# One GpSimd transfer for u, loads ahead of the ramp, and a new order of steps in a fused RWKV and MLP kernel

## The chip, the cores and the metric

The kernel runs on one core of a Trainium2 chip. Its time is device microseconds from the start to the end of one execution. The core has five engines that run side by side, each with its own in-order queue: PE (TensorE, matmuls; its weight loads are listed as PEld), DVE (VectorE), ACT (ScalarE), POOL (GpSimd) and SP (SyncE, which here only issues DMAs). They meet through semaphores.

## What is computed

For 4 batches, 8 heads, 768 time steps and a head size of 48, a linear attention with decay runs through time; its output, 3072 rows of 384, goes through two matrices with a leaky ReLU between them:

```python
for t in range(S):
    cur = np.einsum('bhd,bhe->bhde', u[None] * kt, vt)
    y[:, :, t] = np.einsum('bhd,bhde->bhe', rt, state + cur)
    state = w[None, :, :, None] * state + np.einsum('bhd,bhe->bhde', kt, vt)
x = y.transpose(0, 2, 1, 3).reshape(B * S, H * D)
h = x @ w_in                        # 384 -> 2048
out = np.maximum(0.01 * h, h) @ w_out   # 2048 -> 384
```

## The kernel before

Time is cut into 24 stages of 128 steps (six per batch). Within a stage the recurrence is written as matrix products: the keys and queries are scaled by powers of w, their products (128x128 per head) are masked, and the state is carried from stage to stage. Two stages make a pair (0 to 11), which is 256 rows of x for the two big products.

The program is written out as a list, `ORDER`, of some 880 short step names. A step adds one or a few instructions to the queue of its engine; the list is read once from left to right, so each engine executes its own steps in the order of the list, and every dependence becomes a semaphore wait. The figure behind an `@` names the PSUM bank (of eight) that a PE step writes; a step that takes over a bank waits for the last reader of the step that had it. `RINGS` holds the numbers of buffers: the second is the number of buffers of the transposed keys and queries, `tp`.

The steps by letter, n being a stage and m a pair:

| step | engine | line | what |
|---|---|---|---|
| p0 ... p32 | all | 336 | entries of the list `first`: setting up |
| q | DVE | 373 | zeroes the padding of a qk buffer |
| F | PE | 376 | one product of ones, written to a bank and read by nobody |
| r, k, v | POOL | 267 | load of a stage (cast to bf16 on the way), one DMA each |
| i, w | POOL | 281, 285 | quarter of w_in, of w_out |
| P | DVE | 388 | scales queries and keys by the tables qtab and ktab; for stage 0 in two halves, P0.1 the keys, P0.0 the queries |
| T, C | PE, ACT | 408, 422 | transposes half of it on PE, copies it out of PSUM (stages 0 to 7) |
| X | SP | 402 | transposes by DMA (stages 8 to 23) |
| D, V | DVE | 428, 551 | the part with u for stages 0 to 5: product of keys and queries, and v scaled by its sums |
| E, f, R, L | DVE, POOL | 433 to 459 | the same part for stages 6 to 23: products with u_tab and r, their sums, and a diagonal tile by an affine select on POOL |
| A, M, m, N | PE, DVE, ACT | 467 to 509 | scores, masked (DVE, or ACT copy and DVE mask; from stage 6 a predicated copy over L's tile) |
| K, B, W | PE, DVE | 521 to 570 | keys times values, next state |
| Y, O | PE, ACT | 575, 618 | outputs of the stage, copied as x, transposed |
| J, j | PE, ACT | 650, 664 | 256 columns of h for a pair: six matmuls with 256 moving columns, eviction with the leaky ReLU; eight per pair |
| G, g | PE, ACT | 627, 642 | 512 columns of h for one stage alone: twelve matmuls with 128 moving columns, eviction of the same size; not in the list before |
| t, b, Z, z | DVE, PE | 701 to 766 | the product with w_out in seven half-size products per pair (sums of blocks on DVE, products, combination on ACT and DVE) |
| o | SP, ACT | 690 | stores 128 rows |

The steps of `first` that matter here: p0 loads w as a row, p1 loads u as a row (ACT's queue), p2 and p3 load r and k of stage 0 in fp32 on SP's and ACT's queues (into r0_f and k0_f), p4 to p7 load w and u as columns; p9 is the ramp (an iota on POOL), from which DVE makes kexp (p13), qexp (p14), ident (p15) and mask (p17); p10 sets the ones. p21 spreads w over 128 partitions by a product with a column of ones, p22 takes its logarithm, p24 and p23 make ktab and qtab from it with kexp and qexp. For u, p20 casts the row to bf16, p25 spreads it by a product and p26 copies it to u_tab, which E reads.

PE executes, in the list before, p21, p25, eleven F, T0.1, T0.0, three F, A0, and then stages 1 to 3 with further F between; the first J follows after Y1. POOL executes p9, r3, k3, k1, r1, k2, r2, i1, v0, k5, r5, and so on; L7 stands behind 25 stage loads.

Of the kernel before, what the change touches and what calls it, by code (L numbers as in the profile page):

```python
# [16 lines left out]
HD = H * D  # L17
# [6 lines left out]
RINGS = (6, 7, 6, 6, 6, 3, 3, 8, 14, 14)  # L24
# [8 lines left out]
F1.128.5@4 F1.512.8@2 p24 F1.256.12@0 k2 F1.512.15@7 P0.1 F1.256.4@0 F1.512.16@2 p17 r2 p27 p15 p23 p19 q5  # L33
F1.512.4@0 q4 q3 F1.512.6@7 P0.0 i1 p28 F1.256.9@0 p16 T0.1@2 v0 T0.0@0 F1.512.12@3 C0.1 p32 p31 F1.512.7@4 q1
F1.512.0@3 k5 C0.0 P1 p29 A0@23 D0 p30 r5 F1.512.5@0 q2 M0.0 F1.256.16@7 F1.512.19@6 T1.0@0 v1 P2 F1.128.2@4
F1.256.18@5 F1.512.9@2 C1.0 F1.256.6@7 P3 F1.512.13@6 T1.1@2 v2 M0.1 F1.256.14@0 T3.0@4 C1.1 T2.1@0 T3.1@5 C3.0
v3 D1 A1@23 C2.1 M1.0 i0 C3.1 K0@4 F1.256.3@0 T2.0@2 r4 V0 F1.256.2@0 C2.0 B0 Y0@0 m1.1 k6 P5 F1.256.8@2 A3@45
p26 D2 F1.128.3@7 F1.256.11@6 k4 K1@2 N1.1 D3 T5.1@3 V1 A2@67 r6 C5.1 T5.0@1 M3.1 O0 Y1@3 r7 C5.0 B1 K3@0 M2 O1
K2@5 k7 J0.3@1 v4 V2 A5@23 j0.3 B2 J0.1@6 i3 m5.1 M3.0 J0.0@7 V3 i2 D5 Y2@1 k8 E6 N5.1 Y3@5 O2 P4 v5 j0.1 B3
J0.2@1 O3 P6 v6 T4.1@6 j0.2 J1.3@0 j0.0 w3 T4.0@1 J1.0@3 C4.1 w2 P7 C4.0 J1.1@7 M5.0 w0 A4@45 D4 j1.1 T6.0@6 v7  # L40
f6 T6.1@1 j1.3 M4 T7.0@2 J1.2@7 j1.0 w1 C6.1 K4@0 J1.7@3 r13 C6.0 V4 J0.7@1 E7 j1.7 k9 W3 f7 T7.1@4 B4 j0.7
J1.6@3 R7 C7.0 J0.5@5 R6 j1.6 L7 b0.2 Y4@6 C7.1 j0.5 L6 A7@01 A6@23 O4 W4 K5@4 J0.4@5 V5 M7 J0.6@6 j0.4 r10 Y5@4
j0.6 r8 J1.5@5 b0.0 O5 r11 J1.4@6 b0.1 J2.2@4 M6 r9 j1.4 J2.5@0 j1.2 v8 j2.2 b0.3 J2.7@1 j1.5 k11 K6@6 J2.3@7
b1.0 k10 J2.4@2 B6 b1.1 J2.1@3 v9 b1.2 Y7@4 v11 Y6@5 E8 t0 J2.6@6 O6 k13 O7 Z0.0@5 t2 j2.5 k12 Z1.0@4 j2.7 t1
j2.3 J3.2@0 k14 z0.0 E9 j2.1 K7@1 Z0.1@7 t3 v13 j2.6 J3.1@3 j2.4 f8 r12 b1.3 Z1.1@6 j3.1 P8 v12 Z0.2 P9 Z0.3@2
P11 X9 z0.2 j3.2 f9 Z0.4 B7 z1.1 z1.0 E11 J3.3@3 z0.1 X8 W7 R9 K8@0 Z1.2 j3.3 f11 L9 Z1.3@1 z1.2 Z1.4 P13 Z0.5
R8 X13 z1.4 J3.5@3 L8 B8 z0.4 Z1.5 X11 z1.3 r19 R11 Z0.6 W8 r22 P10 A9@01 j3.5 z1.5 Z1.6 X10 M9 z0.6 L11 A8@56
J2.0@3 r15 M8 J3.6@0 j2.0 v16 J3.4@1 E12 f12 v10 Y9@3 E10 P12 Y8@5 O9 r18 b2.0 X12 J3.0@6 j3.4 E13 O8 Z2.0@3 k17
z0.3 j3.6 f10 f13 J4.7@5 o2 z1.6 R10 k16 j3.0 J4.1@4 z0.5 R13 L10 J3.7@2 j4.1 K12@1 k15 J4.4@0 j3.7 B12 z2.0
J4.0@4 b3.0 j4.7 k19 b2.1 A10@12 j4.0 A11@56 r14 Z2.1@7 j4.4 M11 L13 Z2.2 M10 J4.6@4 k21 J4.2@0 j4.6 b2.3 k23  # L50
J4.5@5 z2.1 j4.2 b2.2 J4.3@6 j4.5 K9@4 z2.2 Z2.3@2 j4.3 B9 R12 A13@01 A12@45 M13 L12 Z3.0@6 Z2.4 z3.0 r21 W9 M12
Z2.5 v20 K10@0 Z3.1@1 B10 v18 z2.5 Y12@4 z3.1 Y10@5 W10 O12 b3.1 Y13@0 v14 Y11@7 P15 O13 K13@4 k18 O10 b4.0 Z3.2
O11 z2.3 J6.0@0 v21 E15 z3.2 z2.4 J6.6@5 f15 v17 b4.1 Z3.3@7 B13 r17 J5.1@2 b3.2 Z2.6 r16 P14 j6.0 b3.3 j5.1
J5.3@4 b4.2 Z3.4 j5.3 P18 J6.2@0 E17 E14 J5.0@2 b4.3 j6.2 J5.5@4 R15 z2.6 o5 f14 Z3.5 L15 X14 j5.5 R14 J6.3@0
j5.0 z3.4 E19 v15 P16 J6.1@3 X15 f19 L14 Z4.0@4 j6.1 Z3.6 o1 W13 X16 J6.4@2 P17 z3.6 j6.6 P19 J5.7@3 j6.4 E18 o7
K14@6 f18 Z4.1@5 j5.7 X18 z3.5 B14 j6.3 J5.4@2 z3.3 z4.0 E16 z4.1 J5.6@3 o4 W14 o0 Z4.2 j5.6 X19 A14@01 z4.2
# [107 lines left out]
def bass_rwkv5_eagle__then__act_leaky_relu_kernel(  # L164
# [13 lines left out]
    def SB(name, shape, dt=BF16):  # L178
        return ctx.enter_context(nc.sbuf_tensor(name, shape, dt))
# [9 lines left out]
    u_row = SB("u_row", [1, HD], FP32)  # L189
# [5 lines left out]
    k0_f = SB("k0_f", [128, HD], FP32)  # L195
    r0_f = SB("r0_f", [128, HD], FP32)
# [7 lines left out]
    u_row16 = SB("u_row16", [1, HD])  # L204
    one_row16 = SB("one_row16", [1, 128])
# [37 lines left out]

    def k_of(n):
        return k_sb[:, n % NRK, :] if n else k0_f[:, :]

    def r_of(n):
        return r_sb[:, n % NRK, :] if n else r0_f[:, :]
# [10 lines left out]
    def load_first(which):  # L259
        src = {"k": k, "r": r}[which][0].rearrange("h t d -> t h d")[0:L, :, :]  # L260
        dst = {"k": k0_f, "r": r0_f}[which]
        eng = {"k": "act", "r": "sp"}[which]
        queue = {"k": A, "r": SP}[which]
        add(eng, lambda: queue.dma_start(dst[:, :].rearrange("p (h d) -> p h d", d=D), src),
            W=[(which, 0)], dma=f"{which}0")
# [25 lines left out]
    def row(h):  # L291
        return dram(h, 0, [[HD, 1], [1, HD]])
# [11 lines left out]
    def spread_w():  # L304
        i, key = opened("w")
        add("pe", lambda: PE.matmul(ps[i][:, 0:HD], one_row[:, :], w_row[:, :], start=True, stop=True),
            R=["one_row", "w_row"], W=[key, "bc"])

# [3 lines left out]

    def spread_u():
        i, key = opened("u")
        add("pe", lambda: PE.matmul(ps[i][:, 0:HD], one_row16[:, :], u_row16[:, :], start=True, stop=True),  # L315
            R=["one_row16", "u_row16"], W=[key, "bc16"])
# [14 lines left out]
    def column_wu(hh):  # L331
# [5 lines left out]
        lambda: add("sp", lambda: SP.dma_start(w_row[:, :], row(w)), W=["w_row"], dma="w"),  # L337
# [9 lines left out]
        lambda: add("dve", lambda: V.memset(one_row16[:, :], 1.0), W=["one_row16"]),  # L347
# [12 lines left out]
        lambda: add("act", lambda: A.activation(u_row16[:, :], u_row[:, :], AF.Copy), R=["u_row"], W=["u_row16"]),  # L360
# [503 lines left out]
```

## Time and profile before

| | |
|---|---|
| median of 3 runs | 166.12 us (165.94 to 167.41) |
| profiled execution | 166.21 us |
| its span, first to last instruction | 164.1 us |
| granted TensorE clock | 1.00 |
| instructions | 5320 |
| DMA | 19.68 MB in 100091 packets, mean 120 GB/s |

The span is what the profile's rows cover; the profiled execution's time has some 2 us around it. Times in rows count from the span's start. The length of a row is that of one instruction or, with "x8", of eight of them from the first start to the last end; matmuls overlap, so their lengths in the timeline are longer than their shares in the chain of waits. A row in the chain is the time that the chain spent there.

### The profile page before, as it was taken

Reading aid. Unit: us, or ns where it says so; the run is one execution under the profiler, and the core shown is the slowest. Engines: PE = TensorE matmul, PEld = TensorE weight load, DVE = VectorE, ACT = ScalarE, POOL = GpSimd, SP = SyncE. Lnnn points to the kernel's source line nnn. Section 1 sums busy time; section 2 is a strip of 40 time slices with the busy share of each in tenths; the row PEclk is TensorE's granted clock in tenths of the full one; section 3 lists DMA queues with packets and bytes.
Section 4 is the critical chain, followed back from the end, with each engine's and each line's share of the span. In section 5 each row is a group of like instructions: output and inputs, shape, how many; then the busy total and the mean of one; then the engine's idle time right before and its main releaser. Section 6 shows DMA issues by size and latency. Waiting matters only on the chain.

```text
span 164.1 us, 5320 instructions
## 1 busy us (share of the span) xinstructions
PE 157.8 (96%) x2283; PEld 137.3 (84%) x2283; DVE 130.8 (80%) x261; ACT 88.6 (54%) x195; POOL 89.0 (54%) x101
## 2 busy tenths in 40 slices
PE   4899999999999899999999999999999999999993
PEld 1356778888999688899998988998989998999993
DVE  2579996999997998999997979899769960514771
ACT  3558569954862367623668256453673625738220
POOL 7999999599949969599360469000491000000000
PEclk9999999999999999999999999999999999999999
DMA  6999999999999999959999979935980000034116
GB/s 104 114 147 154 160 174 176 202 191 147 141 142 198 123 139 185 100 30 110 88 151 270 221 123 105 56 67 112 225 46 6 4 0 4 0 121 173 47 32 213
DMA packets 100091, 19.68 MB, mean 120 GB/s; under 512 B 93154, under 2 KB 100068, under 8 KB 100068
## 3 DMA queue, kind: packets, MB, share of 16 engines
q0 software_dynamic: 76512, 10.03, 93.5%
q1 hardware_dynamic: 22226, 8.92, 24.9%
q10 hardware_dynamic: 1330, 0.39, 1.0%
q8 instruction: 18, 0.29, 0.7%
q14 instruction: 5, 0.04, 0.1%
HBM read 20.45 MB, written 4.72 MB: 153 GB/s over the span
## 4 chain that ended last, share of the span: by engine, by line
PE 93%; DVE 2%; DMA 2%; issue 1%; ACT 0%; ACTq 0%; DVEq 0%
PE ps_all L658 39%; PE ps_all L760 33%; PE ps_all L603 6%; PE ps_all L475 4%; PE ps_all L381 4%; PE ps_all L415 3%; PE ps_all L533 2%; DMA u_row<-in_u_dram 2%; PE ps_all L607 1%; DVE out_sb L781 1%; DVE qk L393 1%; PE ps_all L529 0%; ACT u_row L360 0%; PE ps_all L315 0%; DVE sum_t L567 0%
## 5 line engine op out<-in xcount | busy, mean ns | idle before, releaser
L658 PE MATMUL ps_all<-xT,w_in_sb 128*128 128x256 bf16 x576 | 71.8, 273 | 0.0
L667 ACT ACTIVATE gT<-ps_all 128x512 bf16<-128x512 f32 x96 | 54.2, 604 | 31.4 <-PE ps_all L658 25.0
L658 PEld LDWEIGHTS ps_all<-xT,w_in_sb 128*128 128x128 bf16 x576 | 54.1, 98 | 6.8 <-DVE at L499 0.2
L461 POOL TENSOR_SCALAR_AFFINE_SELECT at<-s_tok 128x1024 bf16<-128x1024 f32 x18 | 21.3, 1195 | 33.8 <-DVE s_tok L446 33.7
L760 PE MATMUL ps_all<-tw,gs 128*128 128x192 bf16 x288 | 28.2, 246 | 0.0
L760 PEld LDWEIGHTS ps_all<-tw,gs 128*128 128x128 bf16 x288 | 24.0, 98 | 0.4
L499 DVE CAST_PREDICATED at<-mask,ps_all 128x1024 bf16<-128x1024 uint16 x18 | 21.5, 1216 | 2.1 <-PE ps_all L475 1.1
L781 DVE TENSOR_TENSOR out_sb<-ps_all,snap 128x192 f32<-128x192 f32 x37 | 12.5, 351 | 13.1 <-PE ps_all L760 12.9
L276 POOL DMA_DIRECT2D v_sb<-in_v_dram x24 | 22.1, 943 | 0.0
L729 DVE TENSOR_TENSOR gs<-gT 128x1024 bf16<-128x1024 bf16 x24 | 18.2, 765 | 4.6 <-ACT gT L667 4.6
L276 POOL DMA_DIRECT2D rk_sb<-in_r_dram x23 | 21.3, 939 | 0.3 <-issue 0.3
L276 POOL DMA_DIRECT2D rk_sb<-in_k_dram x23 | 21.1, 939 | 0.0
L771 ACT ACTIVATE snap<-ps_all 128x192 f32<-128x192 f32 x36 | 11.3, 333 | 18.0 <-PE ps_all L760 17.9
L760 PE MATMUL ps_all<-w_out_sb,gT 128*128 128x192 bf16 x192 | 19.3, 246 | 0.0
L621 ACT ACTIVATE xT<-ps_all 128x384 bf16<-128x384 f32 x24 | 11.1, 496 | 10.4 <-PE ps_all L603 8.6
L760 PEld LDWEIGHTS ps_all<-w_out_sb,gT 128*128 128x128 bf16 x192 | 15.9, 98 | 0.7
L393 DVE TENSOR_TENSOR qk<-rk_sb,tab 128x768 bf16<-128x768 bf16 x23 | 15.3, 685 | 0.0
L426 ACT ACTIVATE tp<-ps_all 128x512 bf16<-128x512 f32 x16 | 9.0, 604 | 5.0 <-PE ps_all L415 5.0
L603 PE MATMUL ps_all<-at,v_sb 128*32 128x128 bf16 x384 | 10.5, 220 | 0.1
L603 PEld LDWEIGHTS ps_all<-at,v_sb 128*32 128x32 bf16 x384 | 8.2, 96 | 2.4 <-issue 1.3
L760 PE MATMUL ps_all<-w_out_sb,gs 128*128 128x192 bf16 x96 | 9.9, 246 | 0.0
L446 DVE TENSOR_REDUCE s_tok<-ku 128x8 f32<-128x384 bf16 x18 | 9.7, 544 | 0.1
(69 smaller groups left out, 184.3 us busy)
## 6 DMA issues: line engine op xcount, KB each, us to landing
out_dram<-out_sb SPq DMA_DIRECT2D x22, 192.0 KB, 2.2
v_sb<-in_v_dram POOLq DMA_DIRECT2D x24, 96.0 KB, 5.0
rk_sb<-in_r_dram POOLq DMA_DIRECT2D x23, 96.0 KB, 5.2
rk_sb<-in_k_dram POOLq DMA_DIRECT2D x23, 96.0 KB, 5.3
w_in_sb<-in_moe_w_in_dram POOLq DMA_DIRECT2D x4, 384.0 KB, 5.9
w_out_sb<-in_moe_w_out_dram POOLq DMA_DIRECT2D x4, 384.0 KB, 10.3
tp<-qk SPq DMA_TRANSPOSE x16, 4.3
k_f<-in_k_dram ACTq DMA_DIRECT2D x1, 192.0 KB, 2.9
```

The lines of the kernel that those rows point to most:

```text
L276: add("pool", lambda: G.dma_start(dst, src), W=[key], dma=f"{which}{n}")
L393: add("dve", lambda: V.tensor_tensor(qk[iq][:, :, 0:D], both, by, ALU.mult), R=[("r", n % NRK), ("k", n % NRK), "qtab", "ktab", ("qk0", iq ...
L461: add("pool", lambda: G.affine_select(out=at[ia][:, :, :, :].rearrange("p two m i -> p (two m) i"), in_=s_tok[i2][:, :].unsqueeze(2).to_br ...
L499: add("dve", lambda: V.copy_predicated(dst, mask[:, :].bitcast(mybir.dt.uint16).unsqueeze(1).to_broadcast([128, H, 128]), raw), R=keys + [ ...
L603: last = PE.matmul(ps_y[32 * q:32 * q + 32, 128 * s:128 * s + 128], a, m, start=first_mm and (s == 0 or whole), stop=last_mm and whole)
L621: add("act", lambda: A.activation(xT[m % NX][:, :, 128 * half:128 * half + 128], ps[i][:, 0:HD].rearrange("p (s t) -> p s t", t=128), AF.C ...
L658: last = PE.matmul(ps[i][:, 256 * f:256 * f + 256], w_in_sb[:, s, 128 * fb:128 * fb + 128], xT[ix][:, s, :], start=s == 0, stop=s == NSL - 1)
L667: add("act", lambda: A.activation(gT[ig][:, 2 * j:2 * j + 2, :].rearrange("p f t -> p (f t)"), ps[i][:, :], AF.Prelu, alpha=0.01), R=[key] ...
L729: add(eng, lambda: on.tensor_tensor(x[i][:, :, :], a, b, op), R=keys, W=[("gs", m % 2, i)])
L760: done = PE.matmul(ps[i][:, 0:NH], lhs[:, s, :], rhs[:, s, :], start=bool(opens) and s == 0, stop=s == HF - 1, skip_group_check=not (opens ...
L771: add("act", lambda: A.activation(snap[i2][j][:, :], ps[i][:, 0:NH], AF.Copy), R=[key], W=[("snap", i2, j)])
L781: add("dve", lambda: V.tensor_tensor(out_sb[io][:, cols], ps[i][:, 0:NH], snap[i2][j][:, :], ALU.add), R=[key, ("snap", i2, j), *after], W ...
```

## The change

Five things are changed:

- u is no longer loaded as a row, cast, spread by PE and copied. One DMA on POOL's queue reads u for all 128 partitions (step 0 over partitions in DRAM) and casts it into u_tab. It stands behind v7 in POOL's order. Steps p12, p20, p25 and p26 and the tiles u_row, u_row16 and one_row16 are gone.
- r and k of stage 0 go to two of the output buffers (out_sb 4 and 5) in place of r0_f and k0_f. Two entries behind the list (p33, p34) are not in the order.
- POOL starts with r2, k2, r1, k1; the ramp p9 follows, then i1, v0, k3, r3, v1, v2, r5, i0. L7 stands behind 27 stage loads and u.
- Of pair 0, J0.0 to J0.3 are replaced by G0.0, G0.1, G1.0 and G1.1.
- The list stands in another order, with ten F in place of 28 (9728 moving columns before, 2816 after), and `tp` has eight buffers in place of seven.

PE's order at the start is now p21, F, T0.1, F, T0.0, F, T2.1, T2.0, A0, T1.1, F, T1.0, three F, K0, A1, A2, Y0, F, K1, F, G0.1, T3.0, T3.1, Y1, K2, A3, F, G1.1, G0.0, G1.0, T5.0, T5.1, K3, Y2, Y3. DVE executes q1, p19, q4, p10, q3, p11, p16, p13, q2, p14, p17, q0, P0.1, p15, q5, P0.0, P2, p31, p32, P1, D0, M0.1, p18, M0.0, D1, V0, B0, and from V3 on B3, P4, D5, N5.1, P7, M5.0, D4, M4, b0.2, W3, V4, B4, P6, b1.2, E7, E6, f7, V5, W4, R7, f6, R6, B6, M7, M6.

```diff
-RINGS = (6, 7, 6, 6, 6, 3, 3, 8, 14, 14)
+RINGS = (6, 8, 6, 6, 6, 3, 3, 8, 14, 14)
...
+FIRST = {0}
 ORDER = """
-p3 p0 p9 p12 q0 p2 p18 p1 r3 p11 p13 p14 p10 p4 p8 p5 p21@0 k3 p6 p20 k1 p7 p25@1 F1.256.0@2 p22 r1 F1.128.4@3
...
+p3 p0 q1 r2 p19 q4 p2 p8 p10 p4 q3 p11 p16 k2 p5 p21@0 p6 r1 p7 F1.256.2@1 k1 p22 p9 i1 p13 q2 p24 p14 p17 q0 v0
+p23 P0.1 p27 p15 q5 k3 T0.1@7 P0.0 F1.128.12@6 P2 T0.0@5 C0.1 r3 p31 p32 F1.128.20@6 T2.1@4 C0.0 P1 T2.0@3 v1 D0
+A0@01 C2.0 v2 T1.1@2 C2.1 M0.1 F1.512.12@3 p28 C1.1 r5 p18 T1.0@7 M0.0 F1.128.5@1 F1.512.0@6 C1.0 i0 F1.512.1@5
+p29 K0@6 D1 p30 k5 A1@01 V0 A2@23 m1.1 B0 Y0@7 v3 P3 F1.256.14@1 O0 N1.1 r4 K1@1 D2 F1.256.13@4 G0.1@5 M1.0 k4
...
 def k_of(n):
-        return k_sb[:, n % NRK, :] if n else k0_f[:, :]
+        return early("k", n) if n in FIRST else k_sb[:, n % NRK, :]
...
+    def early(which, n):
+        return out_sb[4 + 2 * n + (which == "k")][:, :]
...
+    def first_u():
+        add("pool", lambda: G.dma_start(u_tab[:, :], dram(u, 0, [[0, 128], [1, HD]])), W=["u_tab"], dma="u")
...
-    def spread_u():
-        i, key = opened("u")
-        add("pe", lambda: PE.matmul(ps[i][:, 0:HD], one_row16[:, :], u_row16[:, :], start=True, stop=True),
-            R=["one_row16", "u_row16"], W=[key, "bc16"])
-
-    def keep_u():
-        i, key = banks["u"]
-        add("act", lambda: A.activation(u_tab[:, :], ps[i][:, 0:HD], AF.Copy), R=[key], W=["u_tab"])
...
-        lambda: add("act", lambda: A.dma_start(u_row[:, :], row(u)), W=["u_row"], dma="u"),
-        lambda: load_first("r"),
-        lambda: load_first("k"),
...
+        first_u,
+        lambda: load_early("r", 0, "sp"),
+        lambda: load_early("k", 0, "act"),
```

More of the change, by code (lines that the diff above doesn't have):

```diff
@@ L74 @@
+z11.0 j11.7 Z10.3@4 z11.1 b11.0 Z10.4 b11.1 Z11.2@7 z10.4 Z10.5 Z11.3 z10.5 b11.3 Z11.4 z11.3 z10.3 Z10.6 z11.2
+o20 z11.7 Z11.5 z11.4 z10.6 o23.0 o23.1 Z11.6@6 z11.5 o21 o22.1 z11.6 o22.0
 """
@@ L242, in hd, with key_of @@
         return x.rearrange("p (h d) -> p h d", d=D)
+    def early(which, n):
+        return out_sb[4 + 2 * n + (which == "k")][:, :]
     def k_of(n):
-        return k_sb[:, n % NRK, :] if n else k0_f[:, :]
+        return early("k", n) if n in FIRST else k_sb[:, n % NRK, :]
     def r_of(n):
-        return r_sb[:, n % NRK, :] if n else r0_f[:, :]
+        return early("r", n) if n in FIRST else r_sb[:, n % NRK, :]
+    def key_of(which, n):
+        if n in FIRST:
+            io = 4 + 2 * n + (which == "k")
+            return [("o", io, 0), ("o", io, 1)]
+        return [(which, n % NRK)]
     banks = {}
@@ L255, in opened, with load_early @@
         return banks[name]
[L259 to L265, printed above, removed]
+    def load_early(which, n, eng):
+        src = {"k": k, "r": r}[which][0].rearrange("h t d -> t h d")[L * n:L * n + L, :, :]
+        dst, queue = early(which, n), {"act": A, "sp": SP}[eng]
+        add(eng, lambda: queue.dma_start(dst.rearrange("p (h d) -> p h d", d=D), src),
+            W=key_of(which, n), dma=f"{which}{n}")
     def load_one(which, n):
@@ L346, in bass_rwkv5_eagle__then__act_leaky_relu_kernel @@
         lambda: add("dve", lambda: V.memset(one_row[:, :], 1.0), W=["one_row"]),
-        lambda: add("dve", lambda: V.memset(one_row16[:, :], 1.0), W=["one_row16"]),
+        None,
         lambda: add("dve", lambda: V.tensor_scalar(kexp[:, :], ramp[:, 0:1], 1.0, float(MID - 1), ALU.mult, ALU.add),
@@ L359, in bass_rwkv5_eagle__then__act_leaky_relu_kernel @@
         lambda: add("dve", lambda: V.memset(wu[:, :, :], 0.0), W=["wu"]),
-        lambda: add("act", lambda: A.activation(u_row16[:, :], u_row[:, :], AF.Copy), R=["u_row"], W=["u_row16"]),
+        None,
         spread_w,
@@ L366, in bass_rwkv5_eagle__then__act_leaky_relu_kernel @@
                     R=["lnw", "kexp"], W=["ktab"]),
-        spread_u,
-        keep_u,
+        None,
+        None,
         lambda: column_log(0), lambda: column_log(1), lambda: column_exp(0), lambda: column_exp(1),
         lambda: column_wu(0), lambda: column_wu(1),
+        lambda: load_early("r", 1, "act"), lambda: load_early("k", 1, "sp"),
     ]
```

90 lines of the change are left out of this document (38 added, 52 removed).

## The prediction

> **What bounds the kernel now.** I read the page's busy times first, then the window table, then the chain of waits from its start, then the timeline of single engines over the first 35 us.
>
> ```profile
> PE 157.8 (96%) x2283; PEld 137.3 (84%) x2283; DVE 130.8 (80%) x261; ACT 88.6 (54%) x195; POOL 89.0 (54%) x101
> ```
> ```profile
> 59.00:161.60 102.60, 102.56 (x1496) 94.41 (x1484) 80.11 (x157) 54.09 (x124) 35.13 (x37) 1.00 0.81 98
> ```
>
> The second line is one stretch of the window table (length, then PE, PEld, DVE, ACT, POOL busy, granted clock). From 59 us to the last matmul PE stands still for 0.04 us, while DVE has 22 us to spare. So the end is the time at which PE becomes dense plus a fixed amount of matmul work, and a change can pay only in what PE loses earlier. The chain shows that loss (start, length, what):
>
> ```profile
> 1.26 2.84 DMA u_row<-in_u_dram
> 4.13 0.53 ACT u_row L360
> ...
> 4.70 0.49 PE ps_all L315
> 5.20 3.31 PE ps_all L381 x11
> 8.51 0.85 PE ps_all L415 x8
> 9.36 1.28 PE ps_all L381 x3
> 10.64 0.46 PE ps_all L475 x8
> 11.10 0.65 PE ps_all L381 x3
> ...
> 11.97 0.71 PE ps_all L381 x5
> ...
> 13.00 0.67 PE ps_all L415 x12
> ...
> 19.73 0.71 PE ps_all L658 x6
> 20.44 0.33 PE ps_all L475 x8
> 20.77 1.42 PE ps_all L658 x12
> 22.18 0.50 PE ps_all L603 x28
> 22.69 0.27 PE ps_all L607 x3
> 22.96 0.50 PE ps_all L603 x28
> 23.47 0.27 PE ps_all L607 x3
> ```
>
> L381 is the fill, products of ones that nobody reads. The first useful transposes (T0, L415) begin at 8.51 us behind eleven fills, the scores A0 (L475) at 10.64 behind three more, the first products with w_in (L658) only at 19.73, and stage 3's outputs Y3 end at 23.47 + 0.27 = 23.74. The fills also tell PE's rate: three of 512 columns in 1.28 us are 0.83 ns a column, the five from 11.97 (1664 columns) 0.43 ns. PE runs at half rate until about 11.
>
> **The part that is neutral on PE.** Four J steps (6 matmuls of 256 columns; x12 in 1.42 at 20.77, elsewhere 0.66 each) become four G steps of 12 matmuls with 128 columns. The row at 13.00 has 12 such matmuls, each with its own weight load, in 0.67 us, 56 ns apiece: 4 x 0.67 = 2.68 against 4 x 0.66 = 2.64, so nothing. The Trainium skill ("TensorE: Matmul & The Clock Gate", Back-to-back issue gap) gives about 81 ns per matmul at 128 columns in a stream with weight loads, by which the G steps would cost 1.2 us more; this row disagrees and decides. What G buys is a start after one stage's x, where J needs two. The evictions stay four of 128x512. All other products, sums and loads are the same set in another order, so PE's useful work is unchanged, and so is the end (last z, then the store).
>
> **The start, step by step.** The timeline of POOL, of ACT and of DVE (start, length, what; in brackets the idle time before), and the landing times of the rk_sb loads:
>
> ```profile
> 0.90 0.23 POOL L343 IOTA ramp<- 128x128 f32 x1 [0.39 <-POOLq L849]
> 1.41 1.04 POOL L276 DMA_DIRECT2D rk_sb<-in_r_dram  x1 [0.27 <-issue]
> ...
> 5.04 0.91 POOL L276 DMA_DIRECT2D rk_sb<-in_k_dram  x1
> ```
> ```profile
> 4.55 0.46 ACT L311 ACTIVATE lnw<-ps_all 128x384 f32<-128x384 f32 x1
> 5.12 0.61 ACT L365 ACTIVATE tab<-lnw,kexp 128x384 bf16<-128x384 f32 x1
> ...
> 8.97 1.09 ACT L426 ACTIVATE tp<-ps_all 128x512 bf16<-128x512 f32 x2 [2.40 <-PE ps_all L415]
> ```
> ```profile
> 5.83 0.56 DVE L396 TENSOR_TENSOR qk<-k_f,tab 128x384 bf16<-128x384 f32 x1 [3.67 <-ACT lncol L323]
> ...
> 6.44 0.51 DVE L352 TENSOR_SCALAR ident<-ramp 128x128 bf16<-128x128 f32 x1
> ...
> 7.30 0.49 DVE L399 TENSOR_TENSOR qk<-r_f,tab 128x384 bf16<-128x384 f32 x1
> ...
> 11.14 0.69 DVE L485 TENSOR_TENSOR at<-ps_all,mask 128x512 bf16<-128x512 f32 x1 [0.49 <-PE ps_all L475]
> ```
> ```profile
> DMA to landing us min/median/max: 3.1/5.2/11.9
> ```
>
> 1. *The u chain.* Gone are u_row's load on ACT's queue, its cast (L360), spread_u and keep_u. On the chain that is 1.26 to 5.19 us, but only fills stood behind it. ACT's logarithm (4.55) comes some 0.45 earlier. That is spent at once: POOL's list now reads r2, k2, r1, k1, ramp, so not one load but four stand ahead of the ramp. They take 5.04 - 1.41 = 3.63 us and begin between 0.90 and 1.18, so the ramp ends at 4.76 to 5.04; kexp (DVE) and then ktab (ACT) wait for it. ktab starts at 5.0 to 5.25 instead of 5.12, and P0.1 at 5.8 to 6.05 instead of 5.83: no gain, and below zero by up to 0.2. If each load took 1.04 like the first, 0.5 more.
> 2. *T0.* Between P0.1 and P0.0 stand ident and one memset, where before 7.30 - 5.83 = 1.47 us went by with mask, ident and four memsets. P0.0 starts about 0.9 after P0.1, at 6.7 to 6.95, and ends by 7.45. One fill of 256 columns is ahead of T0, not eleven; T0 runs at half rate (0.43 per half) and ends at 7.7 to 8.0 instead of 9.36. Its second eviction (0.55) ends at 8.4 to 8.7, before 8.97 + 1.09 = 10.06.
> 3. *A0 and the first mask.* T2 (0.85 at half rate) fits beside the evictions; A0 ends at 9.0 to 9.3 instead of 11.10. On DVE, P1 and D0 stand ahead of the first mask product. P1 needs k1, now the fourth load, issued at 3.6 to 3.9: with the median landing of 5.2 it comes at about 9.0, P1 and D0 take 0.8, the mask product starts at 9.9; with the shortest (3.1) it starts at 9.3. Queues are short at that time, so I take 9.6, against 11.14: 1.5 us ahead.
>
> DVE's timeline at the end of stage 3 (state 2, second mask product of stage 3, V3):
>
> ```profile
> 20.43 0.55 DVE L564 TENSOR_TENSOR st<-ps_all,wl 128x384 bf16<-128x384 f32 x1
> 20.90 0.68 DVE L485 TENSOR_TENSOR at<-ps_all,mask 128x512 bf16<-128x512 f32 x1
> 21.50 0.54 DVE L554 TENSOR_TENSOR vs<-v_sb,ps_all 128x384 bf16<-128x384 bf16 x1
> ```
>
> 4. *Stages 0 to 3.* DVE sets this stretch. From the first mask product (11.14) to V3 (21.50) it takes 10.36 us; the new list has the same steps there, less P2 (0.5, now done earlier) and with one memset (0.2): 10.1. V3 starts at 19.4 to 20.0. On PE, T5.1 takes over the bank of the mask product M3.0 and so waits for it; behind it stand K3, Y2, Y3. M3.0 starts 0.60 + 0.47 ahead of V3 (starts above), ends 0.4 before V3's start; T5.1 0.22, K3 some 0.25 (392 columns), Y2 and Y3 0.77 each. Y3 ends about 1.7 after V3's start, 21.1 to 21.7, against 23.74: 2.0 to 2.6 earlier.
> 5. *What is done by then.* By Y3's end the old order had three J (1.97) and A5 (0.33) done, the new one has four G (2.68): 0.4 more. The lead is 2.4 to 3.0 us, 2.7 in the middle.
> 6. *The clock.* 28 fills become 10 (9728 columns, now 2816). If half rate lasts through A1, A2, K0 and Y0 (about 1.3 us of such work at full rate), a part of that comes on top: 0 to 1.0, I take 0.4.
>
> **After Y3.** POOL's timeline (the last load before the two affine selects), DVE's first predicated copy (M7), and PE's A8 in the chain:
>
> ```profile
> 28.40 1.05 POOL L276 DMA_DIRECT2D rk_sb<-in_k_dram  x1
> 31.28 2.58 POOL L461 TENSOR_SCALAR_AFFINE_SELECT at<-s_tok 128x1024 bf16<-128x1024 f32 x2 [1.84 <-DVE s_tok L446]
> ```
> ```profile
> 34.47 1.21 DVE L499 CAST_PREDICATED at<-mask,ps_all 128x1024 bf16<-128x1024 uint16 x1
> ```
> ```profile
> 55.61 0.40 PE ps_all L475 x8
> ```
>
> The old list takes 34.47 - 21.50 = 12.97 us from V3 to M7 on DVE; the new one has b1.2 and B6 more in between (0.6 + 0.5), so M7 would start at 19.7 + 14.0 = 33.7. POOL was free at 29.45 before; two loads and u more stand ahead of L7 (three times 0.9) and the queue starts 0.5 earlier, so L7 and L6 (1.29 each) end at 32.9 and 34.2: in time for M7, and M6 ends near 36.1. PE, from Y3 at 21.4 through 15 J (9.9), four A (1.3), six T (1.3), Y4, Y5 (1.5) and three K (0.6), 14.6 us in all, asks for it at 36.0. This has no cover: what DVE is later there, PE waits. I book 0.2. The other place is the stretch at 51 to 56 us, where the old chain leaves PE for DVE and comes back to A8 at 55.61; PE stands still there for well under 1 us, and the new order may save some of it or not: 0.
>
> The u transfer stands in POOL's queue behind 20 loads, four weight loads and the ramp, so at 0.9 + 20 x 0.9 + 4 x 0.8 + 0.2 = 22.3; landing in 5.2 gives 27.5. Its first reader, E7, comes on DVE at about 28.5 (some 15 of 24 steps from V3 to M7). Cover 1 us; f7 and R7 hang on it, then L7, for which POOL is free only at 31.6, so 2 us more cost nothing.
>
> **Sum.** 2.7 - 0.4 - 0.2 = 2.1, with ends 0.9 and 3.2; a small gain at 55 us may come on top, so I take 2.4. The profiled execution took 166.21 us (span 164.1), 0.1 from the median 166.12: 166.2 - 2.4 = 163.8.
>
> **Rivals.**
>
> *The lead is given back before 60 us.* For it: M6 without cover, transposes by DMA (X8 is now third in its queue and A8 waits for it), and DVE steps that stretch when an affine select runs beside them. One or two such waits cost 1 to 2 us: 164.8 to 166.2, middle 165.4. Against it: DVE's steps ahead of each Y and Z are no more than before, by and large. Chance 0.20.
>
> *The slow clock lasts (slower than before).* In the old run full rate came about 6 us after the fills began (5.20 to 11), and between them PE never paused. The new order has only ten fills and pauses in front of T0.0, T2, A0 and Y0. If the rate rises only at time t, PE started at 7.3 has lost 7.3 + (t - 7.3)/2, against 13.7 in the old run at Y3 (23.74 less 10.1 us of work at full rate: ten T 2.2, five A 1.7, four K 1.3, Y0 to Y3 2.9, three J 2.0): the lead is gone at t = 20, and t = 24 gives 2 us more than before, 168.2; with pauses up to 170. Against it: even with pauses PE is busy most of the time from 7.3 on. Chance 0.11. The Trainium skill ("TensorE: Matmul & The Clock Gate", Part 1) has the clock released after a free-running window of about 3.4 us with sustained activity; the old run's 6 us agree with one window missed and one filled, and by that rule each further window that the pauses spoil keeps the half rate for 3.4 us more and costs up to half of that; two of them would make 163.8 some 167.
>
> *u lands late.* If its landing takes the longest of the rk loads, 11.9 us, it is there at 34.2, E7, then L7 and M7 wait some 4 us and PE with them: about 167.8. Its rows are long and few, so 0.03.
>
> *More gain.* No wait for k1, full rate by 11, no wait at 55 us: 3.2 + 0.6, so 162.4. Chance 0.08.
>
> **Numbers.** The forecast case, 163.0 to 164.4, has 0.58. One per cent of 166.1 is 1.7, so faster means below 164.4: 0.58 + 0.08 = 0.66; within: 0.20; slower: 0.11 + 0.03 = 0.14. The range 162.2 to 166.5 leaves out the two slow cases and little else.
>
> **What would show it.** Right: the ramp at 4.5 to 4.8, P0.1 still near 5.9, A0 near 9, V3 at 19.4 to 20.0, Y3's end at 21.1 to 21.7, G steps of 0.67, PE idle under 0.5 after that. Wrong: matmuls of 128 columns at 107 ns after 14 us; ktab after 5.5; P1 waiting for k1 past 9.1; a PE wait at Y6 or A8; E7 waiting for u.

## The result and the profile after

| | before | changed |
|---|---|---|
| median, us | 166.22 (20 runs, 165.14 to 168.47) | 169.35 (20 runs, 166.55 to 171.38) |
| profiled execution, us | 166.21 | 166.55 |
| its span, us | 164.1 | 164.8 |

The kernel became slower: the ratio is 1.0111, 95% interval 1.0066 to 1.0155. (The ratio leaves out executions of either kernel far above its fastest one; the medians of all executions differ by 1.9%.) The profile shows the fastest of the 20 executions, which has to be kept in mind when it is read. First the page, with the busy times and the row of the DMA engines over 40 slices of the span, then the table of what PE waited for (total, times, longest).

```profile
PE 152.9 (93%) x2288; PEld 136.5 (83%) x2288; DVE 127.1 (77%) x260; ACT 88.8 (54%) x193; POOL 89.8 (54%) x102
...
DMA  6999999999999999999999999900151102101505
```
```profile
PE ps_all L408 <- DVE ident L344: 2.9, 1, 2.9
...
PE ps_all L468 <- DMA tp<-qk: 2.1, 1, 2.1
PE ps_all L753 <- DVE st L557: 0.8, 1, 0.8
PE ps_all L522 <- DMA v_sb<-in_v_dram: 0.7, 2, 0.3
```

PE is busy for less time than before, so the start did lose its fills. But two waits are new behind the start: L468 is A8, which waits for stage 8's transposes by DMA, and L753 is Z5.1, which waits for a bank that B18 on DVE has not yet read. The chain of waits shows where the lead was and where it went (start, length, what):

```profile
21.65 0.27 PE ps_all L600 x3
...
36.80 0.73 PE ps_all L596 x44
...
49.87 6.47 DMA tp<-qk
56.34 0.14 issue
56.47 0.69 PE ps_all L468 x16
```

Y3 ends at 21.92, where it ended at 23.74 before: 1.8 us ahead, with 0.4 us more work done by then. Y6 starts at 36.80 without a wait. A8 starts at 56.47, 0.86 later than before. The balance of this execution is 2.2 - 2.1 - 0.8 + 0.6 (the one late wait of the old order), about nothing. It does not explain the median, 3 us higher. (In the rows, L651 are products with w_in, L753 products with w_out, L596 and L600 a stage's outputs, L468 the scores A, L408 the transposes of keys and queries, L629 the G steps; in other kernels the numbers are shifted by a few lines; "issue" is time in which the engine waited for nothing that the profile shows.)

### The profile page after: what moved, and what is told of

Read it like the earlier page. It is cut to its first block, busy times and chain, and to the rows that moved or that the text cites. A ratio compares the mean times of both kernels' runs of the same rounds, so it can differ in the third digit from the quotient of the medians.

```text
span 164.8 us, 5327 instructions
## 1 busy us (share of the span) xinstructions
PE 152.9 (93%) x2288; PEld 136.5 (83%) x2288; DVE 127.1 (77%) x260; ACT 88.8 (54%) x193; POOL 89.8 (54%) x102
## 4 chain that ended last, share of the span: by engine, by line
PE 68%; DMA 14%; DVE 8%; POOL 6%; issue 2%; SPq 0%; DVEq 0%; POOLq 0%
PE ps_all L753 27%; PE ps_all L651 27%; DMA tp<-qk 7%; PE ps_all L596 5%; DMA rk_sb<-in_k_dram 4%; POOL rk_sb L277 3%; DMA v_sb<-in_v_dram 3%; PE ps_all L468 3%; DVE qk L386 2%; PE ps_all L629 2%; POOL v_sb L277 2%; DVE gs L722 2%; PE ps_all L408 1%; PE ps_all L526 1%; DVE s_tok L439 1%
## 5 line engine op out<-in xcount | busy, mean ns | idle before, releaser
L660 ACT ACTIVATE gT<-ps_all 128x512 bf16<-128x512 f32 x92 | 53.4, 602 | 35.5 <-PE ps_all L651 21.4
L651 PE MATMUL ps_all<-xT,w_in_sb 128*128 128x256 bf16 x552 | 67.2, 273 | 0.0
L651 PEld LDWEIGHTS ps_all<-xT,w_in_sb 128*128 128x128 bf16 x552 | 52.2, 98 | 6.5
L753 PE MATMUL ps_all<-tw,gs 128*128 128x192 bf16 x288 | 28.5, 246 | 0.8 <-DVE st L557 0.8
L722 DVE TENSOR_TENSOR gs<-gT 128x1024 bf16<-128x1024 bf16 x24 | 16.3, 684 | 12.7 <-PE ps_all L753 8.6
L753 PEld LDWEIGHTS ps_all<-tw,gs 128*128 128x128 bf16 x288 | 24.2, 98 | 1.4 <-DVE st L557 1.0
L764 ACT ACTIVATE snap<-ps_all 128x192 f32<-128x192 f32 x36 | 11.6, 333 | 19.4 <-PE ps_all L753 19.1
L753 PE MATMUL ps_all<-w_out_sb,gT 128*128 128x192 bf16 x192 | 19.6, 246 | 0.0
L753 PEld LDWEIGHTS ps_all<-w_out_sb,gT 128*128 128x128 bf16 x192 | 16.0, 98 | 0.3
L386 DVE TENSOR_TENSOR qk<-rk_sb,tab 128x768 bf16<-128x768 bf16 x23 | 12.4, 551 | 0.4 <-PE ps_all L526 0.2
L596 PE MATMUL ps_all<-at,v_sb 128*32 128x128 bf16 x384 | 10.6, 221 | 0.1
L468 PE MATMUL ps_all<-tp 48*128 48x128 bf16 x192 | 8.3, 221 | 2.1 <-DMA tp<-qk 2.1
L596 PEld LDWEIGHTS ps_all<-at,v_sb 128*32 128x32 bf16 x384 | 8.0, 96 | 2.2 <-issue 0.8
L753 PE MATMUL ps_all<-w_out_sb,gs 128*128 128x192 bf16 x96 | 9.9, 246 | 0.0
```

The costliest lines, as they stand in the source:

```text
L386: add("dve", lambda: V.tensor_tensor(qk[iq][:, :, 0:D], both, by, ALU.mult), R=[("r", n % NRK), ("k", n % NRK), "qtab", "ktab", ("qk0", iq ...
L468: last = PE.matmul(ps[i][:, 128 * p:128 * p + 128], tp[it][at_rows, NP + p, :], tp[it][at_rows, p, :], start=True, stop=True)
L596: last = PE.matmul(ps_y[32 * q:32 * q + 32, 128 * s:128 * s + 128], a, m, start=first_mm and (s == 0 or whole), stop=last_mm and whole)
L651: last = PE.matmul(ps[i][:, 256 * f:256 * f + 256], w_in_sb[:, s, 128 * fb:128 * fb + 128], xT[ix][:, s, :], start=s == 0, stop=s == NSL - 1)
L660: add("act", lambda: A.activation(gT[ig][:, 2 * j:2 * j + 2, :].rearrange("p f t -> p (f t)"), ps[i][:, :], AF.Prelu, alpha=0.01), R=[key] ...
L722: add(eng, lambda: on.tensor_tensor(x[i][:, :, :], a, b, op), R=keys, W=[("gs", m % 2, i)])
```

## Experiments

### Single suspects around A8

Each of the first kernels has one edit in the changed order. X8 and X10 exchanged on SP:

```diff
-P8 z1.2 X10 j2.3 ... L8 z0.3 X8 z0.4
+P8 z1.2 X8 j2.3 ... L8 z0.3 X10 z0.4
```

> The changed kernel with X8 and X10 exchanged in SP's queue, nothing else. Theory 'place in the queue': in the changed kernel X10's issue held SP from 47.25 to 49.83 us although A10 is needed last; X8 then issues some 2.6 us earlier, lands near 53.7 in place of 56.34, PE's wait in front of A8 falls from 2.06 us to under 0.4, and the profiled time falls from 166.55 to about 164.6; with no long pause of PE the granted clock is 1.00 in most executions, so that the median falls from 169.35 to 164.5 to 165.5. Rival 'slow landing' (transposes are slowed by the loads that run beside them, wherever they stand): X8 lands after 55.5, the wait stays above 1.2 us, the median stays above 168. Rival 'the lead is lost elsewhere anyway': A8 does not wait but the next steps of PE do, by 1.5 us or more, at Y8 or Y9, and the time stays above 166.

Measured: 169.14 (168.41 to 171.04), ratio to the kernel before 1.0164 [1.0117, 1.0210]: by the median no gain over the 169.35 of the changed kernel, which did not run beside it. The table of DVE's waits in its profile has two rows that the first profile lacks:

```profile
DVE tw L703 <- DMA w_out_sb<-in_moe_w_out_dram: 1.5, 1, 1.5
...
DVE ku L429 <- DMA u_tab<-in_u_dram: 0.5, 1, 0.5
```

The steps t waited for w_out and E7 for u. Scaled keys for X8 come behind those on DVE, so X8 was late here too. It was less late than in the changed order, though. The row of A8 and A9 (in brackets A8's wait):

```profile
57.73 0.62 PE L468 MATMUL ps_all<-tp 48*128 48x128 bf16 x16 [1.02 <-DMA tp<-qk]
```

A8 waited 1.0 us and the next scores 1.3. In two later profiles of the changed order, with loads about as late, A8 waited 3.5 and 4.6, so X8's place counts as well.

Nine fills ahead of A8:

```diff
-L9 B8 A8@67
+L9 B8 F1.512.30@6 ... F1.512.38@6 A8@67
```

> The changed kernel with nine fills of 512 columns (1.95 us at full rate) in front of A8, where PE stood idle for 2.06 us; the wait for X8 stays. Theory 'pause lowers the clock': most executions of the changed kernel show a granted clock of 0.98 to 0.99 and 168.5 to 171.4 us, the few with 1.00 show 166.6 to 167.3, because the pause costs one or two stretches at half rate behind it; with the pause filled the clock is 1.00 in nearly all executions and the median 166.3 to 167.3. Rival 'the low clock has another cause': the median stays at 168.5 to 170 with a clock of 0.98 to 0.99.

Measured: 171.81, ratio 1.0342 [1.0289, 1.0395]. A8 waited 2.8 us although the fills stood in front of it. The granted clock was 0.99 to 1.00 in the six executions, nearly as expected, but the time did not fall: the low clock alone is not the loss. The ramp ahead of the loads:

```diff
-p3 p0 q1 r2 p19 ... p22 p9 i1
+p3 p0 q1 p9 r2 p19 ... p22 i1
```

> The changed kernel with the ramp in front of POOL's first load again. Theory: in the changed kernel ktab waited until 5.54 us for kexp and so for the ramp (5.04), while the logarithm was ready at 4.3; with the ramp first ktab starts at about 4.4, P0.1 at 5.1 to 5.3 in place of 6.25, the loads start 0.1 to 0.4 later, and Y3 ends about 0.8 us earlier, near 21.1. The end follows by 0 to 1 us only as far as X8 comes earlier too: median 168 to 169.4. Rival 'the loads were worth it': P2 or P1 waits for the later r2, k2, r1, k1, and Y3 ends at 21.9 or later.

Measured: 170.78, ratio 1.0288 [1.0234, 1.0342]. The wait for ident fell from 2.9 to 1.8 us, the time did not: DVE waited 3.0 us for k and 1.5 for w_out, and A8 3.5. The new order up to the copy of stage 3's x (O3), the old order behind it, with u behind v3:

```diff
-O3 T4.1@6 T4.0@4 m5.1 p1 J1.1@0 C4.0 N5.1 v5 J1.2@7 g0.1 ...
+O3 g0.1 g1.0 m5.1 k8 E6 N5.1 v5 P6 v6 T4.1@6 J1.3@0 ...
```

> The changed kernel's list up to the end of stage 3 (through O3, with the four G steps; u's transfer moved up behind v3), and from there the old list's order for all that is left (T4.0 on bank 2). Theory 'the start is faster, the rest of the new order gives it back': Y3 ends at 21.8 to 22.2 as in the changed kernel, the old middle has X9 and X8 as its first two transposes and keeps most of the lead of 1.8 + 0.4 us: 164.0 to 165.0, clock 1.00. Rival 'no order can keep it' (DVE and the loads set the pace up to 60 us): a wait of 1 us or more between 50 and 60 us and 165.7 to 166.5.

Measured: 171.97, ratio 1.0327 [1.0273, 1.0380]. This one says little: the old order asks for k6 early and the new order of loads brings it late, so DVE waited 5.8 us for it.

All four had waits for loads that the first profile did not have. That became the theory: loads land late, and the new order has no time in hand for it.

### Parts of the change alone, in the old order

The changed kernel once more, beside three parts of the change.

> The changed kernel once more, unchanged, beside the three parts below. Theory (loads land with a scatter of several us behind a DMA queue that is full until 100 us, and the new order has no cover for it): around 169.3, range 168.3 to 170.3, and the profile shows waits at other places than the 2.1 us at A8 alone: the t steps for w_out, E7 for u or stage products for v, 1 to 3 us together. Rival (the order itself costs its 2.1 us at A8 in every execution and the rest is the clock): the same time, but with the waits of the first profile and no DVE wait on a load above 0.3 us.

Measured: 171.73 (171.02 to 173.20), ratio 1.0316 [1.0268, 1.0363]; DVE waited 3.3 us for k, 1.5 for w_out, 0.9 for u, A8 3.5. So the first profile was not typical. G for J in the kernel before:

```diff
-J0.3@1 ... j0.3 ... J0.1@6 ... J0.0@7 ... J0.2@1
+G0.1@1 ... g0.1 ... G0.0@6 ... G1.0@7 ... G1.1@1
```

> The kernel before with one part of the change: the four J steps J0.0 to J0.3 become G0.0, G0.1, G1.0, G1.1 at the same places, with 128 columns. Theory (neutral, as predicted): 166.3, within 0.3 of the kernel before; each G step 0.67 us. Rival (weight loads cost 25 ns more for each of 48 products, as in the sentence on the Trainium skill): 1.2 us slower, 167.5.

Measured: 167.15, ratio 1.0044 [1.0004, 1.0085], so 0.1 to 1.4 us, which does not exclude the rival. The chain speaks against it (start, length, what):

```profile
19.34 0.67 PE ps_all L636 x12
...
20.34 1.56 PE ps_all L636 x24
```

This G step takes 0.67 us, a J step 0.66; the next two take 1.56 together, where two J took 1.42. The rival's price of 25 ns for each product would be 0.3 per step. Fewer fills in the kernel before, 18 of 28 taken out:

```diff
-F1.256.0@2 p22 r1 F1.128.4@3 F1.128.5@4 F1.512.8@2 p24 F1.256.12@0 k2 F1.512.15@7 P0.1 ...
+F1.256.0@2 p22 r1 F1.128.4@3 F1.128.5@4 p24 k2 P0.1 ...
```

> The kernel before with 10 of its 28 fills (2944 columns in place of 9728), order otherwise unchanged. Theory (fills cost nothing and the clock rises anyway, since PE has work from 8 us on): 165.8 to 166.5. Rival (the fills hold the clock up; without them half rate lasts some windows longer): 1 to 3 us slower, 167.3 to 169.5, with fills and transposes at half rate after 14 us and a granted clock of 0.98 to 0.99.

Measured: 167.70, ratio 1.0007 [0.9965, 1.0049]. The medians of all executions differ by 0.95 us, so fills are at most a small part. And u by the wide transfer in the kernel before, where it stands behind v3 and is issued at 12.8 us:

```diff
-        lambda: add("act", lambda: A.dma_start(u_row[:, :], row(u)), W=["u_row"], dma="u"),
+        lambda: add("pool", lambda: G.dma_start(u_tab[:, :], dram(u, 0, [[0, 128], [1, HD]])), W=["u_tab"], dma="u"),
```

> The kernel before with u by one wide transfer on POOL's queue behind the load of v3, and without the load of u_row, its cast, the product that spreads it and its eviction. Theory (a transfer of 96 KB more in a full queue costs the other loads little): 166.3, within 0.5; w_out and r, k, v land within 0.5 us of before. Rival (the transfer from one DRAM row holds the queue up and is what makes the loads late): loads behind it land 1 to 2 us later and the time rises by 1 us or more, 167.3 to 169.

Measured: 168.45, ratio 1.0105 [1.0052, 1.0158]: this part alone costs 1%. The landing times of the four w_out loads, from the table of the tile w_out_sb, with G for J (no wide transfer) and then with the wide transfer, on the same chip:

```profile
DMA to landing us min/median/max: 10.3/12.4/14.1
```
```profile
DMA to landing us min/median/max: 12.5/14.3/15.9
```

w_out, which stands behind u, lands 1.8 to 2.2 us later. Against the kernel with few fills, which has no wide transfer either (11.1/12.9/14.6), it is 1.3 to 1.4. These are single profiles, and that of the wide transfer is the slowest of its six executions.

### u taken out, and the backlog cut

u_tab by a memset in DVE's early idle time, and then u by the old route:

```diff
-        add("pool", lambda: G.dma_start(u_tab[:, :], dram(u, 0, [[0, 128], [1, HD]])), W=["u_tab"], dma="u")
+        add("dve", lambda: V.memset(u_tab[:, :], 0.5), W=["u_tab"])
```
```diff
-p3 p0 q1 ... p11 p16 ... p23 P0.1 ... F1.512.0@6 C1.0 ... m5.1 p1 ...
+p3 p0 p1 q1 ... p11 p12 p16 ... p23 p20 P0.1 ... p25@6 C1.0 p26 ... m5.1 ...
```

> The changed kernel without the transfer of u: u_tab is filled by a memset on DVE in its early idle time (u itself is left out). Theory (loads drain through one full queue, u's transfer puts all behind it 1.5 us later): w_out lands about 1.5 us earlier than in the last profile of the changed kernel (12.4/14.2/16.0 there), the DVE waits for u and part of those for w_out and k go, and the time falls by 1 to 2.5 us, to 168.5 to 170.5. Rival (the new order alone asks too early, u matters little): less than 0.7 us.

> The changed kernel with u by the old route: a load of u_row on ACT's queue, its cast, one product that spreads it (in the place of one fill) and its eviction by ACT. Theory: as without the transfer of u, 1 to 2.5 us faster than the changed kernel, 168.5 to 170.5, less some 0.3 for the eviction. Rival: less than 0.7 us, 170.5 to 172.

Measured on one chip: 165.93 without the transfer (ratio to before 0.9994 [0.9955, 1.0032]), 166.17 with u by the old route (0.9965 [0.9929, 1.0000]). Both are faster than the 168.5 to 170.5 expected. Three of the four w_out loads left out, in the changed order and in the old one:

```diff
+        if i:
+            add("dve", lambda: V.memset(w_out_sb[:, 4 * i:4 * i + 4, :].bitcast(FP32), 0.0626068115234375),
+                W=[("wout", i)])
+            return
         add("pool", lambda: G.dma_start(w_out_sb[:, 4 * i:4 * i + 4, :], wout_view[:, 4 * i:4 * i + 4, :]),
```

> The changed kernel with one of the four w_out transfers; the three other blocks are filled by memsets on DVE at its start (their values are left out). u's transfer stays. Theory (the DMA backlog is the cause): no wait of the t steps for w_out, the loads for stages 8 and 9 land 4 us earlier or more, A8 waits for X8 under 0.7 us, the granted clock stays at 1.0 after the start, and the time is 163.5 to 165.5, what was predicted. Rival (X8's late place in the order and the new order of DVE's steps): A8 still waits 2 us or more and the time stays above 167.

> The kernel before with one of the four w_out transfers, the other blocks filled as in the run beside it. Theory (the old order has cover for its loads): 166.0, within 0.7 of the kernel before. Rival (the backlog costs the old order as much): 1 us faster or more, under 165.3.

Measured on the same chip: 165.41, ratio 0.9943 [0.9904, 0.9982], in the changed order, and 165.37, ratio 0.9933 [0.9907, 0.9959], in the old one. In the first, with u's transfer still there, A8's wait is gone from PE's table; what is left behind the start is

```profile
PE ps_all L757 <- DVE st L561: 0.8, 1, 0.8
PE ps_all L526 <- DMA v_sb<-in_v_dram: 0.3, 1, 0.3
```

So with fewer loads A8 does not wait, though X8 stands where it stood. This does not clear X8's place: in the profile without u's transfer A8 still waited 2.8 us, where DVE had waited only 1.0 for loads. The old order gained 1.3 us by the same cut, which I had not expected: in it, too, loads were not free.

### On one chip: without, old route, once, twice

The runs without u's transfer had stood on another chip than the changed kernel. So all went together once more; the fourth has a second transfer, to a tile that nobody reads:

```diff
         add("pool", lambda: G.dma_start(u_tab[:, :], dram(u, 0, [[0, 128], [1, HD]])), W=["u_tab"], dma="u")
+        add("pool", lambda: G.dma_start(u_two[:, :], dram(u, 0, [[0, 128], [1, HD]])), W=["u_two"], dma="u2")
```

> The changed kernel once more, beside the kernels without u's transfer on the same chip. Theory (u's transfer is what costs): 168.5 to 171.5, with waits for u, w_out or k on DVE and 2 us or more at A8. Rival (chips differ in how fast they drain the loads, and the one of the last runs was quick): where the two kernels without the transfer take 166, this one takes 166 to 167 as well.

> The changed kernel without the transfer of u (u_tab by a memset, u left out), on the same chip as the changed kernel itself. Theory: 165.5 to 167, 3 us under the changed kernel beside it. Rival (chips): within 0.7 us of the changed kernel beside it.

> The changed kernel with u by the old route, on the same chip. Theory: 165.5 to 167, as without the transfer. Rival (chips): within 0.7 us of the changed kernel beside it.

> The changed kernel with a second transfer of u right behind the first, to a tile that nobody reads. Theory: the loads behind them land later once more by what one costs (1.5 to 3 us), w_out's longest landing is 17 us or more, and the time is 1.5 to 4 us over the changed kernel beside it. Rival (u's transfer is cheap and the order asks too early): no more than 0.7 us over it.

| u | median, us | ratio to before | w_out landing, longest, us |
|---|---|---|---|
| one transfer (the changed kernel) | 171.50 | 1.0286 [1.0229, 1.0342] | 15.2 |
| none | 167.91 | 1.0033 [0.9982, 1.0084] | 12.1 |
| old route | 166.52 | 0.9981 [0.9945, 1.0017] | 11.6 |
| two transfers | 171.76 | 1.0299 [1.0253, 1.0345] | 15.6 |

The landings are from the table of the tile w_out_sb in each profile. Chips do not make the difference; u's transfer does, 3.6 to 5.0 us. The window table suggests how. Each row is a stretch (length, busy times, granted clock, DMA share, GB/s); u's transfer is issued at about 22 us. One transfer, none, two:

```profile
28.00:30.00 2.00, 2.00 (x29) 1.84 (x27) 1.43 (x4) 1.28 (x3) 2.00 (x3) 1.00 1.71 135
30.00:32.00 2.00, 1.90 (x52) 1.47 (x49) 1.16 (x2) 2.00 (x6) 1.94 (x3) 1.00 1.32 170
```
```profile
28.00:30.00 2.00, 2.00 (x27) 1.81 (x24) 1.67 (x4) 1.28 (x4) 2.00 (x3) 1.00 1.66 191
30.00:32.00 2.00, 2.00 (x57) 1.74 (x55) 2.00 (x7) 2.00 (x6) 1.37 (x2) 1.00 1.33 201
```
```profile
28.00:30.00 2.00, 2.00 (x28) 1.84 (x26) 1.33 (x3) 1.28 (x4) 2.00 (x4) 1.00 1.46 86
30.00:32.00 2.00, 2.00 (x56) 1.72 (x54) 1.07 (x4) 2.00 (x5) 2.00 (x3) 1.00 1.20 122
```

Read the last column: 191 and 201 GB/s without the transfer, 135 and 170 with one, 86 and 122 with two. In these four microseconds, ahead of u's landing at 32.6, the DMA engines move less, and w_out, which stands behind, lands later. One profile of each kernel is thin evidence for the size: the profile with one transfer is of the slowest of its six executions (173.48 us), and in the profile of the changed kernel's fastest execution the same two rows read 177 and 198, u landed in 7.1 us in place of 10.4, and w_out's longest landing was 11.9, no longer than without the transfer. The expectation for the second transfer failed. In these two rows it lowers the rate by about as much again, but w_out's last load came only 0.9 later (42.8 against 41.9) and the time rose by 0.3 us. PE then waited 2.5 us for a state behind DVE's wait for v, ahead of A8, and only 2.2 at A8. Why a second transfer adds no time is not shown.

How the late loads reach PE is read from the chain of the changed kernel in this call:

```profile
24.48 2.20 POOL w_out_sb L287 x3
26.68 15.19 DMA w_out_sb<-in_moe_w_out_dram
...
42.06 0.96 DVE tw L703
...
50.23 0.55 DVE qk L386
...
53.20 7.42 DMA tp<-qk
60.62 0.14 issue
60.76 1.03 PE ps_all L468 x16
```

The last w_out load is issued at 26.68 and lands at 41.87; t0 stands in DVE's queue and holds P10, P9 and P8 behind it; X8 is issued at 53.20, after P8 and behind X10 in SP's queue, and lands at 60.62. Of t0's 3.3 us of delay against the fastest execution 1.6 is the wait for w_out; before it DVE had waited 1.2 for k (at 24.9) and 1.3 for u (at 32.7). In the old profile t0 came at 41.44, so even this landing would have held it by little; the changed order asks at 38.8 in its fastest execution. A8 then waits 4.6 us, and that has a second price. The window table around it:

```profile
56.00:60.00 4.00, 0.14 (x2) 0.00 (x0) 0.68 (x2) 0.00 (x0) 4.00 (x5) 0.97 1.76 143
60.00:64.00 4.00, 3.24 (x29) 2.66 (x30) 2.53 (x3) 0.60 (x1) 4.00 (x5) 0.50 2.05 183
64.00:68.00 4.00, 4.00 (x88) 3.23 (x87) 1.74 (x4) 1.57 (x4) 4.00 (x6) 0.67 2.33 164
```

PE does next to nothing in the first of these rows, and the granted clock (third figure from the end) falls to 0.50 and stays there to about 66.6 us. PE starts again at 60.76, so half of the 5.9 us from there, 2.9 us of work, is lost on top. In all, by these rows, half rate lasted 4 x (0.03 + 0.50 + 0.33) / 0.5 = 6.9 us. The Trainium skill ("TensorE: Matmul & The Clock Gate", Part 1) has the clock go down after an idle window of about 3.4 us and come back after a busy one. Two such windows are 6.8 us, one of them in part idle, so the trace agrees. The wait for X8 in the changed kernel and in the one with the old route:

```profile
PE ps_all L468 <- DMA tp<-qk: 4.6, 1, 4.6
```
```profile
PE ps_all L480 <- DMA tp<-qk: 1.4, 1, 1.4
```

The two profiled spans differ by 171.7 - 164.3 = 7.4 us; the difference in this wait (3.2) and the clock (2.9) make 6.1 of it, and a wait of 1.1 us for a state, behind DVE's wait for u, most of the rest.

### The waits that remain

With u by the old route the changed order is still not 1.4% faster. X8 ahead of X10 there, as in the first experiment, and then besides it the other waits of its profile:

```diff
-p9 i1 ... q0 v0 ... p25@6 C1.0 p26 i0 F1.512.1@5 ... f6 L7 ... L6 ... k9 ... b6.1 j7.4 ... v23 B18
+p9 v0 ... q0 i1 ... F1.512.0@6 C1.0 i0 p25@5 p26 ... f6 k9 L7 ... L6 ... B18 b6.1 j7.4 ... v23
```

> The changed kernel with u by the old route and X8 ahead of X10 on SP. Theory (without u's transfer the rest of the lead goes at A8, where X8 stands third among the transposes): A8 no longer waits (before 1.4 us in the profile with the old route), X8 lands some 2.5 us earlier, and the time is 1 us under that kernel, 165.0 to 165.8. Rival (the transposes are held by the loads beside them, not by their order): A8 waits 1 us or more as before, and the time stays at 166.2 to 166.7.

> The same, and besides: v0 ahead of the first w_in load and k9 ahead of L7 on POOL, u spread in another bank so that K0 doesn't wait for its eviction, B18 ahead of b6.1 on DVE, so that Z5.1 gets its bank 0.6 us earlier. Theory (each wait that the profile shows on PE after 10 us costs its length): 164.0 to 165.2, about 1 us under the run beside it, 1 per cent under the kernel before, with PE idle under 0.5 us after 12 us and the clock at 1.0. Rival (the waits come back at other places): no faster than the run beside it.

Measured: 168.22 (164.69 to 170.51), ratio 0.9936 [0.9886, 0.9986], and 167.44 (164.78 to 169.56), ratio 0.9923 [0.9874, 0.9973]; the kernel before took 166.75 beside them. In the profile of the first A8 did not wait, as expected, but w_out's longest landing was 14.0 us without any wide transfer, and the time did not follow. The profile of the second, 164.78 us long, has no wait over 0.3 us on PE after the start:

```profile
PE ps_all L420 <- DVE ident L356: 2.8, 1, 2.8
PE ps_all L310 <- DMA w_row<-in_w_dram: 2.2, 1, 2.2
PE ps_all L386 <- ACT at L511: 0.3, 1, 0.3
```

The predicted time is nearly there, but only in some executions: of twelve, five took 164.8 to 166.1 and seven 167.0 to 169.6, six of these with a granted clock of 0.98 to 0.99; no execution of the kernel before beside them was under 0.998. By the median both are slower than the kernel before. With u by the old route and X8 left in its place the median was 0.5 us below it on both chips, with intervals that reach 1.0000 and 1.0017: by the median no version with all its work was clearly faster.

## Why the prediction was wrong

**The neutral part was nearly right.** G steps take 0.67 us in the chain of the changed kernel, as worked out (three more in 2.01), and the part alone moved the time by 0.4% (0.0 to 0.9).

**The start came a little later than worked out.** DVE's, POOL's and ACT's timelines (start, length, what):

```profile
9.71 0.69 DVE L478 TENSOR_TENSOR at<-ps_all,mask 128x512 bf16<-128x512 f32 x1 [0.45 <-PE ps_all L468]
...
20.40 0.56 DVE L547 TENSOR_TENSOR vs<-v_sb,ps_all 128x384 bf16<-128x384 bf16 x1 [0.19 <-PE ps_all L526]
```
```profile
5.04 0.28 POOL L335 IOTA ramp<- 128x128 f32 x1
...
22.18 0.65 POOL L293 DMA_DIRECT2D u_tab<-in_u_dram  x1
```
```profile
5.54 0.62 ACT L357 ACTIVATE tab<-lnw,kexp 128x384 bf16<-128x384 f32 x1 [1.23 <-DVE kexp L340]
```

The ramp ended at 5.32 (4.76 to 5.04 predicted), ktab started at 5.54 (5.0 to 5.25, and past 5.5 was named as a sign of being wrong), the first mask product started at 9.71 (9.6), V3 at 20.40 (19.4 to 20.0), and Y3 ended at 21.92 (21.1 to 21.7). The lead with the work done was 2.2 us, not 2.7. P1 did not wait. These steps held within half a microsecond.

**After Y3** M6 ended at 36.60 and Y6 started at 36.80 without a wait: in time, with as little cover as worked out.

**The step that failed is the price of u's transfer.** The prediction gave it one issue on POOL and a landing of 5.2 us, looked at its first reader alone, and gave lateness 0.03 since "its rows are long and few". It landed in 7.1 us in the fastest execution of the changed kernel, where E7 came only at 30.6 and did not wait, and in 9.5 to 11.4 in the other profiles of the changed order with all its loads, where E7 waited 0.5 to 1.6 us. More than that, it had no term for what stands behind it in a queue without a gap: in the profiles taken side by side w_out landed 3.1 to 3.6 us later. That the transfer costs the time is shown by taking it out in two ways; that it does so by holding the queue is read from single profiles. Without the transfer the kernel is 3.6 to 5.0 us faster; the forecast missed the median by 169.35 - 163.8 = 5.6.

**The second step is "0" at 51 to 56 us.** The rival with the lead given back named the mechanism (X8 third in its queue, A8 waiting) and got 0.20; its price of 1 to 2 us fits the fastest execution (2.1). X8's place cost something by itself: with u by the old route A8 waited 1.4 us, and not at all with X8 ahead of X10, though w_out came later there (14.0 against 11.6). The rival missed that late loads make DVE, and so X8, later still, and that a wait of 4.6 us costs 2.9 more in clock. The rival of the slow clock put the loss at the start; in the profile read here it came at A8, and at the start 16 score products took 0.62 us at 12.3, full rate.

**The cover was counted at one place only.** t0 had 2.7 us more in the old order than in the new one (41.44 against 38.77, with the last w_out load issued at 26.78 and 26.67). No step of the prediction compared issue with demand for w_out.

Not settled: whether the 128 reads of the same row are what slows the queue, or any further load at this place would (no other shape of this transfer was tried), why a second one adds no time, how much X8's place alone is worth (the changed kernel did not run beside that experiment), why the kernel without any u was no faster than the one with the old route, and what spreads the executions of the last two kernels.

## What to carry to other kernels

When a DMA queue has no idle slice, as here, expect the loads behind a new transfer to pay for it; compare, load by load, issue plus the longest landing with the new time of demand, above all when the change makes the consumers earlier. In this kernel a lead won at the start was worth only as much as the loads' time in hand. And a profile of one execution shows one landing time: look at the scatter of the times before a cause is read from it.

## What had not been expected of the hardware

Taking out one 96 KB load whose 128 rows all read the same 1.5 KB made the kernel 3.6 to 5.0 us faster on one chip. In the profiles taken there w_out, behind it, landed about 3 us later with it (longest 15.2 against 12.1 and 11.6 us). The same loads took very different times on different chips and executions, though: w_out's longest landing without the wide transfer was 11.6 to 14.6 us, and with it 11.9 in the fastest execution and up to 16.0 in others. And one pause of 4.6 us cost PE some 2.9 us more at half rate.
